# Strided rows loaded as two separate halves, fourteen weight tiles, and one memory for both score arrays

## The chip, the core and the metric

The kernel runs on one core of one Trainium2 chip. A core has five engines with their own instruction queues: TensorE (PE, with its weight loads as PEld), VectorE (DVE), ScalarE (ACT), GpSimd (POOL) and SyncE (SP). Data move between HBM and the on-chip SBUF through 16 DMA engines that all queues share. The metric is the device time of one execution in microseconds (us). Before the change it is 444.04 us, the median of four runs (443.17 to 445.94).

## The reference

```python
def _attn_ref(q, k, v):                      # 8 batches, 8 heads, 576 positions, 64 wide
    scores = scale * np.matmul(q, k.transpose(0, 1, 3, 2))
    rel = pos[:, None] - pos[None, :]
    mask_local = (rel >= 0) & (rel < 32)
    mask_strided = (rel >= 0) & (pos[None, :] % 32 == pos[:, None] % 32)
    masks = np.stack([mask_local if h < H // 2 else mask_strided for h in range(H)])
    ...
    return np.matmul(softmax(scores), v)

def _moe_ref(x, w_r, w_i, w_ch):             # x: the attention, 8 x 576 x 512
    X = np.fft.rfft(x, axis=1)
    ...
    # for each of 64 modes: Y = X (w_r + i w_i), with 512 x 512 matrices
    y = np.fft.irfft(Y, n=S, axis=1)
    u = x + y
    return u + np.maximum(u @ w_ch, 0.0)
```

Heads 0 to 3 attend to the last 32 positions ("local"), heads 4 to 7 to positions that are a multiple of 32 away ("strided"). The result goes through a Fourier transform, 64 complex 512 x 512 matrices (one for each mode), the inverse transform and one more matrix. All inputs are float32; the mode matrices alone are 134 MB, and the page counts 163.37 MB read from HBM.

## The kernel before

The kernel computes in 16-bit floats. Every load of q, k, v and of the mode matrices is a DMA that POOL issues and that turns float32 in HBM into float16 in SBUF. In the trace POOL has at most eight such DMAs under way: each names one of eight semaphores in turn, and waits for the DMA that used it before. SBUF destinations are tiles from pools with a fixed number of buffers, so an issue also waits until the tile's former contents have been read. POOL works its instructions strictly in order.

There are four stages.

1. **Strided heads**, batches 0 to 7. `load(i)` (L194) takes a buffer `qn` of three (tag `qn`) and fetches v, q and k of heads 4 to 7: 72 rows (4 heads x 18 blocks of 32 positions), each of 2048 numbers. The loop at L718 calls `load(b + 3)`, then `w_fetch` for some mode matrices, then the work of batch b: `str_front` of the next batch (transposes of 128 columns of `qn` by PE, `str_q` and `str_turn`, copies by DVE and ACT), `str_scores` (PE scores, ACT exponentials into the array `PS`), and `str_values` (PE, then `normalise` on DVE). `PS` is cleared once at L714.
2. **Local heads**, batches 0 to 7, with the same buffers `qn` (128 rows of 1152 numbers a load). The exponentials go into the array `PL`, which must be zero between the parts that are written; it is cleared at L734 after strided batch 1. Between pieces of this work stand the first halves of modes, `mode(0, m)`.
3. **Second halves of the modes**, `mode(1, m)`, with the work on the output matrix in between.
4. **Output**: the inverse transform, the last matrix, the additions and the stores.

A mode needs a tile `wt` (128 x 2048), filled by two DMAs of 64 rows, one from `w_r` and one from `w_i` (L180). `w_fetch` takes the next tile in order. There are `NWBUF` = 12 tiles in the pool `pw`; six tiles (numbers 3 to 6, 16 and 17) lie as guests in memory that other arrays use later. Before stage 2 the kernel fetches 2 tiles and then 3, 3, 2, 2, 2, 2, 1, 1 in the eight strided batches, 18 in all. After that each mode fetches one tile as soon as it is done (L523), except the modes whose tile was a guest in the first half. In the output stage the same pool gives the buffers `rl` and `osb`.

Of the kernel before, what the change touches and what calls it, by code (L numbers as in the profile page):

```python
# [11 lines left out]
F16 = mybir.dt.float16  # L12
# [11 lines left out]
JG = [(0, 6), (6, 11), (11, 16)]  # L24
SCALE = float(1.0 / np.sqrt(D))
NEG = -30000.0
NWBUF = 12


def _host_consts():  # L30
# [47 lines left out]
def kernel(  # L78
# [10 lines left out]
    nc = tc.nc  # L89
# [16 lines left out]
    def psum(kind, half=False):  # L106
        if half:
            return pss[kind].tile([128, 1024], F16, tag=kind, name=kind)
        return pss[kind].tile([128, 512], FP, tag=kind, name=kind)
# [27 lines left out]
    def spectra_tile(n):  # L137
        if n == "X0":
            Xh[0] = big.tile([128, 4, B, 2, NM], F16, tag=n, name=n)
        else:  # L140
            YS[n] = big.tile([128, 4, 4, 16, 16], F16, tag=n, name=n)

    xb = [px.tile([128, 11, 256], F16, tag="xb", name="xb") for _ in range(B)]

    pw = ctx.enter_context(tc.tile_pool(name="pw", bufs=NWBUF))
    actx = ctx.enter_context(ExitStack())
    pin = actx.enter_context(tc.tile_pool(name="pin", bufs=3))
    pat = actx.enter_context(tc.tile_pool(name="pat", bufs=1))
# [1 line left out]
    qTs = [pat.tile([128, 1152], F16, name=f"qT{i}") for i in range(2)]  # L150
    kzs = [pat.tile([128, 2, 1216], F16, name=f"kz{i}") for i in range(2)]
    vT = pat.tile([128, 1216], F16, name="vT")
    PS = pat.tile([128, 2342], F16, name="PS")
    PL = pat.tile([128, 4160], F16, name="PL")
    v16 = [pat.tile([128, 12, 132], F16, name=f"v16_{i}") for i in range(2)]


# [7 lines left out]
    def w_fetch(n=1):  # L165
        for _ in range(n):
            i = len(w_tiles)
            if i >= 2 * NM:
                return
            half, m = 1 - i // NM, i % NM  # L170
            if i in GUEST:
                n, j = GUEST[i]
                if j == 0:
                    guests[n] = big.tile([128, 2, 4, DM], F16, tag=n, name="wt")
                wt = guests[n][:, j]
            else:
                wt = pw.tile([128, 4, DM], F16, tag="w", name="wt")

            for ri, src in enumerate([moe_w_r, moe_w_i] if m else [moe_w_r]):
                nc.gpsimd.dma_start(  # L180
                    wt[ds(64 * ri, 64)],
                    src[m, ds(256 * half, 256), :].rearrange("(p c) e -> p c e", c=4),
                )
            w_tiles.append(wt)
# [4 lines left out]
        w_chs["n"] = w_ch  # L189


    qns = {}

    def load(i):  # L194
        if i >= 2 * B:
            return
        qn = pin.tile([128, 3, 2048], F16, tag="qn", name="qn")
        for vi, src in ((2, v), (0, q), (1, k)):
            if i < B:
                nc.gpsimd.dma_start(  # L200
                    qn[0:72, vi, :],
                    src[i, 4:8].rearrange("h (c r) d -> (h c) (r d)", r=32),
                )
            else:
                nc.gpsimd.dma_start(
                    qn[:, vi, 0:1152],
                    src[i - B, 0:4].rearrange("h (cb i) d -> (h cb) (i d)", i=18),
                )
        qns[i] = qn


    def v_cols(i):
        return ds(1 + 65 * i, 65)
# [13 lines left out]
    def act_copy(out, in_):  # L227
        nc.scalar.activation(out=out, in_=in_, func=ACTF.Copy)  # L228
# [4 lines left out]
    def str_q(b, g):  # L233
        qn, qT = qns[b], qTs[b % 2]
        tp = psum("tp", half=True)
        for i in range(8):
            nc.tensor.transpose(
                tp[:, ds(72 * i, 72)],
                qn[0:72, 0, ds(128 * (8 * g + i), 128)],
                idn[0:72, 0:72],  # L240
            )
        nc.vector.tensor_copy(
            out=qT.rearrange("p (h r c) -> p r h c", h=4, r=16)[:, ds(8 * g, 8)],
            in_=tp[:, 0:576].rearrange("p (r h c) -> p r h c", h=4, c=NCB),
        )

    def str_turn(b, vi, j):
        qn = qns[b]
        a, z = JG[j]
        nr = z - a  # L250
        tp = psum("tp", half=True)
        for i in range(nr):
            nc.tensor.transpose(  # L253
                tp[:, ds(72 * i, 72)],
                qn[0:72, vi, ds(128 * (a + i), 128)],
                idn[0:72, 0:72],
            )

        def move(eng, dst, pr):
            eng(  # L260
                out=dst[:, ds(72 * a, 72 * nr)].rearrange(
                    "p (h c r) -> p h c r", h=4, r=nr
                ),
                in_=tp[pr, 0 : 72 * nr].rearrange("p (r h c) -> p h c r", h=4, c=NCB),
            )

        if vi == 2:
            move(act_copy if j else nc.vector.tensor_copy, vT[:, 0:1152], ds(0, 128))
            return
        for rp in range(2):  # L270
            pr = ds(64 * rp, 64)
            move(
                act_copy if j == 1 else nc.vector.tensor_copy,
                kzs[b % 2][pr, rp, 0:1152],
                pr,
            )
# [29 lines left out]
    def str_scores(b, t):  # L306
# [13 lines left out]
        for h in range(4):  # L320
# [7 lines left out]
        nc.scalar.activation(  # L328
            out=PS[0:n, ds(POFF[t], 4 * n)],
            in_=scp[0:n, 0 : 4 * n],  # L330
# [4 lines left out]
    def str_values(b, t):  # L335
        vg = v16[b % 2]
        j, rp = STR[t]
        n = (JG[j][1] - JG[j][0]) * NCB
        avp = psum("av")
        av = avp[:, 0:264].rearrange("p (h c) -> p h c", c=66)  # L340
        for h in range(4):
            nc.tensor.matmul(
                av[:, h, 0:65],
                PS[0:n, ds(POFF[t] + n * h, 128)],
                vg[0:n, 4 * j + h, v_cols(rp)],
                start=True,
                stop=True,
            )
        normalise(
            av[0:n, :, ds(1 - rp, 64)],  # L350
            av[0:n, :, 64 * rp],
            n,
            4,
            xb[b][0:n, 3 * rp + j, :].rearrange("p (c h q) -> p h c q", c=4, h=4),
        )
# [49 lines left out]
    def loc_scores(b, h, tail):  # L405
# [18 lines left out]
        for i, (col, s0, n) in enumerate(todo):  # L424
# [6 lines left out]
            )  # L431
        PV = PL[:, 0:4096].rearrange("p (h x) -> p h x", h=4)
        if tail:
# [7 lines left out]
    def loc_values(b, h):  # L441
        vg = v16[b % 2]
        av = psum("av")[:, 0:330].rearrange("p (t c) -> p t c", c=66)
        for t in range(5):
            off = 1024 * h + (256 * t if t < 4 else 960)
            nc.tensor.matmul(
                av[:, t, 0:65],
                PL[:, ds(off, 128)],
                vg[:, 2 * t + h % 2, v_cols(h // 2)],
# [3 lines left out]
            if t > 0:  # L453
                nc.tensor.matmul(  # L454
                    av[:, t, 0:65],
                    PL[:, ds(1024 * h + 256 * t - 128, 128)],
                    vg[:, 2 * (t - 1) + h % 2, v_cols(h // 2)],
# [11 lines left out]
    def dft(b, half):  # L469
        if half == 0 and b == 0:  # L470
            spectra_tile("X0")
        xp = psum("sc" if half else "y")
        tiles = (
            [(t, (JG[t % 3][1] - JG[t % 3][0]) * NCB) for t in range(6)]
            if half
            else [(t, SCS[t]) for t in range(5)]
        )
        F = cs["cFs"] if half else cs["cFl"]
        base = 0 if half else 6
        for cp in range(2):  # L480
            for i, (t, n) in enumerate(tiles):
                nc.tensor.matmul(  # L482
                    xp[:, ds(192 * cp, 192)],
                    xb[b][0:n, base + t, ds(128 * cp, 128)],
                    F[0:n, t, :],
                    start=(i == 0),
                    stop=(i == len(tiles) - 1),
                )
        xv = xp[:, 0:384].rearrange("p (c x) -> p c x", c=2)
        X = Xh[half]  # L490
        for src in range(2):
            for dst in range(2):
                args = dict(
                    out=X[ds(64 * dst, 64), ds(2 * src, 2), b].rearrange(
                        "p c g m -> p c (g m)"
                    ),
                    in_=xv[ds(64 * src, 64), :, ds(64 - 64 * dst, 128)],
                )
                act_copy(**args)
# [179 lines left out]
    load(1)  # L679
    const_load(nc.sync, "cMl", "cFl", "cA")  # L680
    load(2)
    w_fetch(2)

# [22 lines left out]
    for i, w in enumerate(first):  # L706
# [6 lines left out]
        if i == 2:  # L713
            nc.vector.memset(PS, 0.0)  # L714
        if i == 5:
            nc.vector.memset(kzs[1], 0.0)
    SPLIT = [0, 2, 4, 5, 7, 8, 10]
    for b in range(B):  # L718
        load(b + 3)
        w_fetch([3, 3, 2, 2, 2, 2, 1, 1][b])  # L720
        front = str_front(b + 1) if b + 1 < B else loc_front(0)
        for t in range(6):
            str_scores(b, t)
            if b > 0:
                if t < 2:
                    str_values(b - 1, 4 + t)
                elif t == 2:
                    dft(b - 1, 1)
            if t >= 2:
                str_values(b, t - 2)  # L730
            for w in front[SPLIT[t] : SPLIT[t + 1]]:
                w()
        if b == 1:
            nc.vector.memset(PL, 0.0)  # L734
    str_values(B - 1, 4)
    str_values(B - 1, 5)
    dft(B - 1, 1)


# [179 lines left out]
    for i in range(len(units)):  # L919
        v_rows(i)  # L920
        b, t = units[i]
# [42 lines left out]
```

The softmax here doesn't subtract the row's maximum and nothing guards it: scores larger than these inputs give would overflow.

## Time and profile before

| | |
|---|---|
| median of four runs | 444.04 us (443.17 to 445.94) |
| the profiled execution | 445.94 us; its span, from the first to the last instruction, 444.1 us |
| PE, DVE, ACT, POOL busy | 77%, 49%, 43%, 41% of the span |
| mean granted TensorE clock | 0.801 |
| strided loads (L200) | 24 DMAs of 72 rows of 4096 B each |
| local loads (L205) | 24 DMAs of 128 rows of 2304 B each |
| weight loads (L180) | 254 DMAs of 64 rows of 4096 B each |

The sizes are those written to SBUF; twice as much is read. The profile's page divides the span into 40 slices of 11.1 us and gives the busy share of each engine in tenths, the mean busy share of the 16 DMA engines, and the rate in GB/s as written. A DMA share can be a little above 1 in the windows, since successive packets of an engine overlap. The chain of waits follows the work that ended last back from the end, and gives for each step what released it; time in which an engine waited for a transfer is put down to that transfer.

### The profile page before, as it was taken

The numbers are of one execution on the slowest core, as the hardware profiler recorded it, in microseconds if no ns is written. First come the engines' busy times: TensorE is split into PE (matmuls) and PEld (weight loads), VectorE is DVE, ScalarE is ACT, GpSimd is POOL, SyncE is SP. The second block draws the span as 40 slices with busy tenths as digits, with TensorE's granted clock in tenths as the row PEclk, the third lists the DMA queues.
The fourth block names the chain that finished last, engine by engine and source line by source line (L and its number), as shares of the span: only waits on it lengthen the run. The fifth ranks groups of instructions, "written<-read, shape, count | busy, mean of one in ns | idle before, by whom it ended". The sixth has DMA issues, their size and how long they took to land.

```text
span 444.1 us, 12290 instructions
## 1 busy us (share of the span) xinstructions
PE 341.8 (77%) x5284; PEld 244.1 (55%) x5284; DVE 215.8 (49%) x462; ACT 188.9 (43%) x353; POOL 180.6 (41%) x327
## 2 busy tenths in 40 slices
PE   3887787869979897876865566768587958997994
PEld 2766676758767775654653344445455535554441
DVE  4788776833535425150511033354345443763895
ACT  2686676743545554343341302133222402433882
POOL 5243343332544343434443444444344444410883
PEclk9998897975887959595885559596867768988998
DMA  8999999999999999999999999999999999991687
GB/s 186 183 204 205 196 199 208 209 208 206 165 211 211 212 212 211 212 211 213 212 211 212 211 212 212 213 212 213 211 200 213 212 211 211 212 203 21 261 318 274
DMA packets 30902, 92.35 MB, mean 208 GB/s; under 512 B 5952, under 2 KB 6848, under 8 KB 30848
## 3 DMA queue, kind: packets, MB, share of 16 engines
q0 software_dynamic: 26608, 81.28, 93.6%
q1 hardware_dynamic: 3440, 9.50, 5.7%
q8 instruction: 42, 0.69, 0.6%
q10 hardware_dynamic: 800, 0.77, 0.6%
q14 instruction: 12, 0.10, 0.1%
HBM read 163.37 MB, written 9.44 MB: 389 GB/s over the span
## 4 chain that ended last, share of the span: by engine, by line
DMA 57%; PE 27%; DVE 9%; issue 4%; ACT 2%; DVEq 0%; POOL 0%; POOLq 0%
DMA wt<-in_moe_w_i_dram 40%; DMA wt<-in_moe_w_r_dram 9%; DMA qn<-in_q_dram 4%; PE y L515 4%; PE sc L613 3%; DMA qn<-in_v_dram 3%; DMA qn<-in_k_dram 2%; PE v L860 2%; DVE xb L218 2%; PE tp L363 2%; PE v L648 2%; PE u L663 2%; DVE kz L260 2%; PE sc L409 1%; PE sc L482 1%
## 5 line engine op out<-in xcount | busy, mean ns | idle before, releaser
L515 PE MATMUL y<-X,wt 128*128 128x16 f16 (+1 forms) x2048 | 82.9, 192 | 62.5 <-DMA wt<-in_moe_w_i_dram 58.0
L180 POOL DMA_DIRECT2D wt<-in_moe_w_r_dram x128 | 66.2, 517 | 129.6 <-DMA wt<-in_moe_w_r_dram 35.0
L515 PEld LDWEIGHTS <-wt 128*128 128x128 f16 (+1 forms) x2048 | 72.9, 103 | 75.4 <-issue 55.2
L180 POOL DMA_DIRECT2D wt<-in_moe_w_i_dram x126 | 65.1, 517 | 64.9 <-DMA wt<-in_moe_w_i_dram 39.4
L622 ACT ACTIVATE v<-sc 128x512 f16<-128x512 f32 x32 | 18.9, 597 | 88.7 <-PE sc L613 88.6
L613 PE MATMUL sc<-w_cp,xT 128*128 128x512 f16 (+1 forms) x160 | 52.8, 461 | 0.5 <-DVE xT L585 0.4
L439 ACT ACTIVATE PL<-sc 128x480 f16<-128x480 f32 (+1 forms) x48 | 27.6, 579 | 39.2 <-PE sc L425 39.0
L623 DVE COPY xo<-tp 128x512 f16<-128x512 f16 x32 | 22.1, 692 | 41.4 <-PE tp L621 41.4
L218 DVE TENSOR_TENSOR xb<-av,rec 90x256 f16<-90x256 f32 (+2 forms) x80 | 36.0, 450 | 2.7
L217 DVE RECIPROCAL rec<-av 90x4 f32<-90x4 f32 (+2 forms) x80 | 14.7, 184 | 45.1 <-PE av L454 31.5
L370 DVE COPY qT<-tp 128x576 f16<-128x576 f16 x16 | 12.0, 758 | 44.9 <-PE tp L363 40.7
L228 ACT ACTIVATE v<-tp 128x640 f16<-128x640 f16 (+1 forms) x24 | 19.4, 808 | 28.9 <-PE tp L397 26.0
L363 PE MATMUL tp<-cI_s,qn 64*64 64x64 f16 x864 | 25.9, 209 | 2.1 <-issue 1.0
L873 POOL TENSOR_TENSOR rl<-rl,xo 128x512 f32<-128x512 f32 x16 | 18.3, 1157 | 20.2 <-ACT rl L871 19.5
L328 ACT ACTIVATE PS<-sc 90x360 f16<-90x360 f32 (+1 forms) x48 | 22.8, 488 | 8.2 <-PE sc L321 7.6
L890 DVE TENSOR_TENSOR osb<-u,rl 128x512 f32<-128x512 f32 x36 | 23.8, 689 | 3.1 <-ACT rl L871 1.4
L363 PEld LDWEIGHTS <-qn 64*64 64x64 f16 x864 | 20.4, 121 | 7.4 <-issue 4.4
L253 PE MATMUL tp<-cI_s,qn 72*128 72x72 f16 x256 | 15.1, 209 | 11.8 <-DMA qn<-in_v_dram 9.4
L409 PE MATMUL sc<-cMl_s,cI_s 128*128 128x480 f16 (+1 forms) x48 | 22.5, 470 | 1.6 <-ACT X L228 1.6
L482 PEld LDWEIGHTS <-xb 108*128 108x128 f16 (+2 forms) x176 | 17.0, 114 | 11.4 <-DVE xb L218 5.7
L613 PEld LDWEIGHTS <-xT 128*128 128x128 f16 (+1 forms) x160 | 14.8, 111 | 15.0 <-issue 7.4
L565 DVE COPY xT<-tp 128x512 f16<-128x512 f16 x16 | 11.0, 689 | 24.3 <-DMA wt<-in_moe_w_i_dram 15.2
(94 smaller groups left out, 660.0 us busy)
## 6 DMA issues: line engine op xcount, KB each, us to landing
wt<-in_moe_w_r_dram POOLq DMA_DIRECT2D x128, 256.0 KB, 9.5
wt<-in_moe_w_i_dram POOLq DMA_DIRECT2D x126, 256.0 KB, 9.7
out_dram<-osb SPq DMA_DIRECT2D x14, 512.0 KB, 2.7
qn<-in_v_dram POOLq DMA_DIRECT2D x16, 288.0 KB, 10.3
qn<-in_q_dram POOLq DMA_DIRECT2D x16, 288.0 KB, 10.7
qn<-in_k_dram POOLq DMA_DIRECT2D x16, 288.0 KB, 10.8
out_dram<-osb SPq DMA_DIRECT2D x7, 128.0 KB, 2.5
out_dram<-osb SPq DMA_DIRECT2D x3, 256.0 KB, 2.6
```

The source lines that it names most:

```text
L180: nc.gpsimd.dma_start(wt[ds(64 * ri, 64)], src[m, ds(256 * half, 256), :].rearrange("(p c) e -> p c e", c=4),)
L218: nc.vector.tensor_tensor(out=dst, in0=val.rearrange("p h (q c) -> p h c q", c=4), in1=rec[0:n, 0:pieces] .to_broadcast((n, pieces, 64)) . ...
L228: nc.scalar.activation(out=out, in_=in_, func=ACTF.Copy)
L328: nc.scalar.activation(out=PS[0:n, ds(POFF[t], 4 * n)], in_=scp[0:n, 0 : 4 * n], func=ACTF.Exp, scale=SCALE,)
L363: nc.tensor.transpose(tp[ds(64 * hp, 64), ds(64 * i, 64)], qn[ds(64 * hp, 64), vi, ds(64 * (9 * g + i), 64)], idn[ds(64 * hp, 64), ds(64 * ...
L409: nc.tensor.matmul(scp[:, 0 : n * times].rearrange("p (h x) -> p h x", h=times), idn, mask_rows("cMl", n, times), start=True, stop=False,)
L439: nc.scalar.activation(out=dst, in_=src, func=ACTF.Exp, scale=SCALE)
L482: nc.tensor.matmul(xp[:, ds(192 * cp, 192)], xb[b][0:n, base + t, ds(128 * cp, 128)], F[0:n, t, :], start=(i == 0), stop=(i == len(tiles) ...
L515: nc.tensor.matmul(yv[:, mi, e, :], wt[pr, XC[c], ds(128 * e, 128)], Xh[half][pr, c, :, :, m], start=(c == 0), stop=(c == 3),)
L613: nc.tensor.matmul(vp[pr, :], xT[:, ch, cols], w_chs["cp"][:, ch, :], start=(ch == 0), stop=(ch == 3),)
L623: nc.vector.tensor_copy(out=xo[pr].rearrange("p (h q c) -> p h q c", h=2, c=4), in_=tp[pr, 0:512].rearrange("p (h c q) -> p h q c", h=2, c=4),
L890: nc.vector.tensor_tensor(out=osb[:, t % 2, :], in0=up, in1=rls[b, t][:, t % 2, :], op=AluOp.add)
```

## The change

It has three parts. A strided row of 2048 numbers is no longer one piece: the buffer `qn` grows from 2048 to 2080 columns, and the second half of a row starts at column 1040 in place of 1024, so that the two halves don't adjoin in SBUF. The load's pattern is now 72 x 2 x 1024, and `pair_cols` gives the transposes their columns. The pool of weight tiles has 14 buffers, and batches 6 and 7 of the strided stage fetch two tiles each in place of one; 20 tiles are fetched before stage 2. `PS` is no array of its own but the last 2342 columns of `PL`: the clearing at L734 covers only the first 1818 columns, and a second one clears the others after the last strided values.

```diff
-NWBUF = 12
+NWBUF = 14
...
-    PS = pat.tile([128, 2342], F16, name="PS")
+
     PL = pat.tile([128, 4160], F16, name="PL")
+    PS0 = 4160 - 2342
+    PS = PL[:, ds(PS0, 2342)]
...
+    HALF = 1024 + 16
     qns = {}
+
+    def pair_cols(i):
+        return ds(HALF * (i // 8) + 128 * (i % 8), 128)
...
-        qn = pin.tile([128, 3, 2048], F16, tag="qn", name="qn")
+        qn = pin.tile([128, 3, 2 * HALF], F16, tag="qn", name="qn")
...
-                    qn[0:72, vi, :],
-                    src[i, 4:8].rearrange("h (c r) d -> (h c) (r d)", r=32),
+                    qn[0:72, vi, :].rearrange("p (f x) -> p f x", f=2)[:, :, 0:1024],
+                    src[i, 4:8].rearrange("h (c f r) d -> (h c) f (r d)", f=2, r=16),
...
-                qn[0:72, 0, ds(128 * (8 * g + i), 128)],
+                qn[0:72, 0, pair_cols(8 * g + i)],
...
-                qn[0:72, vi, ds(128 * (a + i), 128)],
+                qn[0:72, vi, pair_cols(a + i)],
...
-        w_fetch([3, 3, 2, 2, 2, 2, 1, 1][b])
+        w_fetch([3, 3, 2, 2, 2, 2, 2, 2][b])
...
-            nc.vector.memset(PL, 0.0)
+            nc.vector.memset(PL[:, 0:PS0], 0.0)
     str_values(B - 1, 4)
     str_values(B - 1, 5)
+    nc.vector.memset(PS, 0.0)
     dft(B - 1, 1)
```

In the order of the instructions nothing else moves: PE has the same instructions in the same order, DVE has the one memset more, and POOL issues the two added tile fetches (four DMAs) ahead of the loads of local batches 2 and 3.

## The prediction

> **What bounds the kernel now.** I read the page's slices first, then the chain of waits, then the windows by stage, then the POOL timeline where a stage lost transfer time.
>
> ```profile
> DMA  8999999999999999999999999999999999991687
> GB/s 186 183 204 205 196 199 208 209 208 206 165 211 211 212 212 211 212 211 213 212 211 212 211 212 212 213 212 213 211 200 213 212 211 211 212 203 21 261 318 274
> q0 software_dynamic: 26608, 81.28, 93.6%
> ...
> DMA wt<-in_moe_w_i_dram 40%; DMA wt<-in_moe_w_r_dram 9%; DMA qn<-in_q_dram 4%; PE y L515 4%; PE sc L613 3%; DMA qn<-in_v_dram 3%; DMA qn<-in_k_dram 2%; PE v L860 2%; DVE xb L218 2%; PE tp L363 2%; PE v L648 2%; PE u L663 2%; DVE kz L260 2%; PE sc L409 1%; PE sc L482 1%
> ```
>
> From slice 2 to slice 36 the DMA engines are at 90% or more, and the chain that ends last lies for 40 + 9 + 4 + 3 + 2% of the span in transfers that POOL issues. In order of time the chain runs through DMA from 50 to 73 us (the strided rows of the last batches), through the compute engines from 73 to 134, through weight transfers from 134 to 373, and from 373 through the last modes and the output stage, 71 us that follow the weights of mode 51 whenever those land. So the time is the 16 engines' transfer work up to about 373 us, plus whatever they lose before that. The windows (columns: busy PE, PEld, DVE, ACT, POOL; granted clock; DMA share; GB/s) show where they lose:
>
> ```profile
> 20.00:30.00 10.00, 8.27 (x149) 6.80 (x147) 8.65 (x25) 8.16 (x19) 3.13 (x7) 1.00 1.04 202
> 50.00:60.00 10.00, 7.54 (x114) 6.52 (x113) 6.66 (x19) 6.34 (x15) 3.75 (x8) 0.83 1.03 195
> 110.00:114.00 4.00, 4.00 (x95) 3.90 (x92) 1.93 (x5) 1.73 (x3) 1.78 (x4) 0.52 0.67 125
> 260.00:330.00 70.00, 52.22 (x679) 33.80 (x679) 27.97 (x55) 14.92 (x26) 27.88 (x55) 0.75 1.06 212
> ```
>
> Weights alone run at 212 GB/s. The stage with strided rows (up to 70 us) runs at 195 to 206, and at 110 to 114 us the rate falls to 125.
>
> **Part 1: the strided rows.** Each of the 24 strided loads has 72 rows of 4096 B. The page's packet count says how they are dealt out. Queue 0 has 26608 packets. Data rows are 254 x 64 weight rows, 24 x 72 strided, 24 x 128 local and 512 of `w_ch`: 21568. The 5040 left are completion packets of 4 B. 303 DMAs with 16 engines each make 4848; the other 192 are 24 x 8. So every strided load carries eight fillers: 72 + 8 = 80 = 16 x 5. The trace's landing records agree: of a load's 16 increments two come early (the first q load: 4.88 and 6.13 us) and fourteen together (7.90 to 8.41 us). Fourteen engines take five rows, one takes two, one none, and the loaded engines set the pace. In the packet records successive packets on one engine start 304.5 ns apart at 4096 B, 173 at 2304 and 79 at 1024; these lie on a line of 73.4 ns per 1000 B plus 3.9 ns, so 2048 B is estimated at 154.2 ns.
>
> After the change a load is 144 pieces of 2048 B. If the 144 are dealt out as the 72 were, each engine gets exactly nine. Per load the busiest engine goes from 5 x 304.5 = 1522.5 to 9 x 154.2 = 1387.8 ns, 134.7 less, times 24 loads = **-3.2 us**. The whole is on the path if the engines had no other cause of idling then; for the first nine loads (start and constants) that is not clear, so the smaller bound is 15 x 134.7 ns = 2.0.
>
> Here the Trainium skill speaks against the change ("DMA: Bandwidth & Descriptors", "Why a DMA increments its semaphore by 16 and not by 1"): the number of engines comes from the slowest dimension, and some copies from GpSimd get 16 engines with partitions/16, rounded up, on each. The row agrees for 72 x 1, where pieces and partitions are the same, and can't tell them apart. Read by partitions, 72 x 2 still gives five partitions, ten pieces, to fourteen engines: 10 x 154.2 = 1542 ns, 24 x 19.5 = +0.5 us in place of -3.2. I take dealing by pieces, because the fillers pad the pieces to a multiple of 16 and the pattern has no other trace of partitions; both ends stay in the range.
>
> POOL's side: an issue takes 526 ns for 72 rows, 531 to 566 for 128, 782 for the 512 pieces of `w_ch`, so about 570 for 144: 24 x 40 ns = 1 us of POOL. It lies beside POOL's own waits for earlier transfers (the view of waits: 50 us each before `w_r` and `w_i` issues), so nothing; without that cover, 1 us. The transposes read other columns at the same count and width: nothing.
>
> **Part 2: two more weight tiles.**
>
> ```profile
> 104.25 0.52 POOL L180 DMA_DIRECT2D wt<-in_moe_w_i_dram  x1
> 111.76 0.52 POOL L180 DMA_DIRECT2D wt<-in_moe_w_r_dram  x1 [6.99 <-PE y L515]
> ```
>
> This is the hole at 110 us. By 97 us all 18 tile slots (12 and six guests) are filled; modes 3 to 6 free guest tiles and fetch nothing, so POOL issues nothing for 7 us and the queue runs dry. The loss is 4 x (1 - 125/212) = 1.6 us. With 14 tiles two more fetches (batches 6 and 7) stand ahead of the hole: 4 DMAs x 4 rows per engine x 304.5 = 4.9 us of work. Part 1 takes 3.2 us from the same queue, so it runs dry 1.7 us later, about the size of the hole; if PE reaches mode 7 earlier, because the strided rows came earlier, the cover is better. I take **-1.5 us** (bounds 0.5 and 1.6; up to 0.9 more if the 179 GB/s just behind the hole, 114 to 120 us, is its consequence). Total bytes are the same: the two tiles come earlier, not additionally. What is late next: from 134 us on the weights again; PE does a mode of the local stage in some 1.7 us (22 modes from 97 to 134) against 2.4 us of transfer, so it eats the lead and then waits as before.
>
> Queued behind the two fetches are POOL's loads of local batches 2 and 3 (issued at 86.4 and 94.0). They slip by 2.4 and 4.9 us less what part 1 gives, and land near 100 and 109 us; their transposes start in the rounds of local batches 1 and 2, after 112 us: nothing. The pool is also that of the output stage's `rl` and `osb`; no row of the waits has these waiting for an output transfer, so two more buffers give nothing there.
>
> **Part 3: the scores' shared memory.** The memset at L734 shrinks from 1.79 us (2080 words) to 1818/4160 of it, 0.78; on DVE in batch 1, a stretch in which the chain goes on to wait for DMA at 50 us, so nothing. A memset of 1171 words is added after the last strided values: 1.03 us by the row of the same memset at L714 (7.84 us). It starts behind the last normalise (94.4 + 0.4 us) and ends near 95.9; the first local exponential, which now waits for it, runs at 98.32 because its scores wait for the copies of X, and DVE's next instruction comes at 98.95 after 4.1 idle us. So 0; uncovered, 1.0 us.
>
> **Sum.** -3.2 - 1.5 + 0 = -4.7 us. The profiled execution took 445.94 (span 444.1 and 1.8 around it), so it would take 441.2. It is the longest of the four; against the median of 444.04 the forecast is **439.3 us**, -1.1%.
>
> **Rivals.** (a) *Dealt by partitions.* Part 1 is +0.5, the hole is covered in full: -1.6 + 0.5 = -1.1, so 442.9, which can't be told from no change. For it: the skill's wording. Against: the fillers. (b) *Twelve engines.* The other branch of the same rule gives 72 rows the largest divisor up to 16, which is 12; today's loads don't follow it, but two-dimensional ones might. Then a used engine gets 12 pieces, 1850 ns. If the twelve move on from load to load, the mean is nine again and the forecast holds. If they are always the same, each load costs 328 ns more than now: 24 x 0.328 = +7.9, less 1.6: 450.3, slower. It decides from the point where the busiest engine's share of a load exceeds 1522.5 + 1640/24 = 1591 ns, that is 10.3 pieces. Nothing in today's loads speaks for it; the one two-dimensional load, `w_ch`, has 128 partitions and does not tell. The same point is reached if 2 KB pieces cost over 177 ns each, which the 173 ns of 2304 B speaks against. (c) *The loads stay hidden*: if compute sets the pace to 134 us, balance only fills buffers sooner. But that is what the two tiles absorb, and from 134 us the time is transfer work; without it only part 2 would remain, 442.5.
>
> **The numbers.** Forecast, with moving twelves, 0.63; (a) with (c) 0.25; (b) and other losses 0.12. What can be told from no change is 0.5%, 2.2 us: below 441.8 is faster. The forecast's own range is 437.5 to 441.5 (-3.0 to -5.7, and a run's scatter), so nine tenths of it are faster; of (a) a fifth. Faster 0.57 + 0.05 = 0.62, slower 0.12, the rest 0.26. Range 437.5 to 443.8: up through (a) and its scatter, leaving out (b).
>
> **What would show it.** Dealing: queue 0 would have 16256 + 3456 + 3072 + 512 + 4848 = 28144 packets without fillers; 28528 with sixteen per load says (a). The windows from 20 to 70 us should rise from 195-206 to about 210 GB/s, and the two early increments of each load go. The hole: no window of 4 us under 200 GB/s between 105 and 120, and no 7 us of idle POOL that empties the queue. The last weights should land near 397 instead of 402 us, with the 42 us behind them unchanged. A strided stage that is no faster than now would make the first step wrong; a hole that only moves would make the second wrong; local exponentials that wait for DVE, the third.

## The result and the profile after

| | before | after |
|---|---|---|
| median | 444.13 us (64 runs, 442.58 to 446.66) | 444.49 us (43 runs, 441.54 to 448.75) |
| profiled execution | 445.94 us, span 444.1 | 445.08 us, span 443.3 |
| PE, DVE, ACT, POOL busy | 77%, 49%, 43%, 41% | 77%, 49%, 42%, 42% |

The ratio of the times after and before is 1.0008, with a 95% interval of 0.9997 to 1.0018: no change that can be told. The forecast was 439.3 us. The longest of the 43 runs, 448.75 us, counts as a slow one and is left out of the ratio. These are the lines of the changed kernel's page that answer to those shown before:

```profile
DMA  8999999999999999999999999999999999990687
GB/s 172 182 192 204 203 204 208 211 212 212 212 211 213 210 210 201 211 209 215 210 213 209 211 211 213 212 213 210 211 193 211 211 212 212 211 207 15 262 320 274
q0 software_dynamic: 29296, 81.29, 95.3%
...
DMA wt<-in_moe_w_i_dram 44%; DMA qn<-in_v_dram 5%; DMA qn<-in_q_dram 5%; DMA wt<-in_moe_w_r_dram 4%; PE y L524 4%; PE sc L622 3%; PE v L870 2%; PE v L657 2%; DVE xb L227 2%; PE tp L372 2%; PE u L672 1%; DVE kz L269 1%; PE sc L491 1%; PE sc L418 1%; PE sc L434 1%
```

Three things are to be seen. The slice that stood at 165 GB/s (the eleventh, 111 to 122 us) is at 212: the hole is gone. The first four slices, which held 186 183 204 205, hold 172 182 192 204, and the next two, which held 196 199, hold 203 204: the start got slower, and the rest of the strided stage hardly faster. And the queue has 29296 packets, neither the 28144 nor the 28528 that the prediction had named. The chain is of the same make as before, with 44 + 5 + 5 + 4% of the span in transfers that POOL issues; the transfers still set the end. The windows of the changed kernel (busy PE, PEld, DVE, ACT, POOL; granted clock; DMA share; GB/s) say the same more sharply:

```profile
10.00:20.00 10.00, 7.03 (x83) 6.22 (x84) 6.50 (x11) 4.11 (x8) 3.54 (x6) 1.00 1.27 178
20.00:70.00 50.00, 41.88 (x674) 35.36 (x672) 38.81 (x108) 35.59 (x78) 21.27 (x37) 0.90 1.12 200
110.00:114.00 4.00, 4.00 (x70) 3.49 (x68) 1.37 (x4) 1.79 (x4) 1.51 (x3) 0.66 1.08 214
260.00:330.00 70.00, 52.82 (x678) 33.89 (x674) 28.29 (x56) 15.28 (x26) 27.39 (x54) 0.71 1.06 211
```

The kernel before, in the same stretches:

```profile
10.00:20.00 10.00, 8.34 (x117) 7.28 (x116) 6.88 (x16) 5.65 (x10) 3.11 (x6) 1.00 1.07 184
20.00:70.00 50.00, 39.20 (x658) 32.79 (x656) 39.64 (x107) 36.15 (x80) 18.53 (x37) 0.93 1.04 201
```

From 20 to 70 us the rate is the same, 200 against 201 GB/s, but the DMA share rose from 1.04 to 1.12. The share counts the time for which packets are open; for the same bytes they are open longer. The records of the single packets agree: 2048 B has a median of 173 ns (successive starts 154 ns apart, as estimated), but a mean of 196 ns, and in the microseconds behind each group of strided loads the mean of one microsecond peaks at 220 to 284 ns.

**How the loads are dealt out.** By size, the queue's packets are 16256 of 4096 B, 3456 of 2048 B, 3072 of 2304 B, 512 of 1024 B and 6000 of 4 B. 303 DMAs with 16 completions each make 4848 of the small ones; 1152 are left, 48 for each of the 24 strided loads. 48 = 4 x 12: four engines get twelve 4-byte fillers each, and twelve engines get 144 / 12 = 12 pieces. The landing records agree: of the first v load's 16 increments four come at 4.76 to 5.24 us, and twelve at 6.45 to 8.52. An increment does not name its engine, but engines that are left out every time run ahead: in the kernel before, two of the increments of the seventh load come at 7.40 and 11.10 us and fourteen at 17.30 to 18.07. In the changed kernel all sixteen of the seventh load come at 17.04 to 19.20, so the twelve move on. That is the other branch of the rule that the prediction quoted from the Trainium skill ("DMA: Bandwidth & Descriptors", "Why a DMA increments its semaphore by 16 and not by 1"): the largest number up to 16 that divides the slowest dimension, here 12 of 72, on consecutive engines from a cursor that goes round. The count of twelve and the moving on agree with it; no run here shows that the engines are consecutive. The loads of the kernel before (72 x 1) follow its exception instead, rounded-up shares on 16 engines, with their eight fillers. In both cases the fillers bring every engine up to the largest share: 3 + 5 where one engine has two rows of five and one has none, 4 x 12 here.

**What this did at the start.** The first strided loads landed later: v at 8.5 us in place of 6.2, q at 11.3 in place of 8.4, and the first exponential runs at 17.4 in place of 14.6. The lead of the transfers over those of the kernel before (difference of the bytes of queue 0 begun so far, at 212 GB/s) was -0.7 us at 5 us, -1.5 at 40 and -0.4 at 110. It became +1.25 at 114 and +2.2 at 120 through the hole that is no longer there, and +0.8 at 372; 0.6 and 0.5 us of it went at about 172 and 326 us, where POOL stops (last section). The profiled execution before was 1.8 us longer than its kernel's median and this one 0.6 longer than its own, so the small lead left at the end fits a ratio of 1.

### The profile page after: what moved, and what is told of

It reads as the page before. It is cut to its first block, busy times and chain, and to the rows that moved or that the text cites. A ratio compares the mean times of both kernels' runs of the same rounds, so it can differ in the third digit from the quotient of the medians.

```text
span 443.3 us, 12287 instructions
## 1 busy us (share of the span) xinstructions
PE 339.1 (77%) x5284; PEld 242.6 (55%) x5284; DVE 216.0 (49%) x463; ACT 188.2 (42%) x353; POOL 184.9 (42%) x327
## 3 DMA queue, kind: packets, MB, share of 16 engines
q0 software_dynamic: 29296, 81.29, 95.3%
## 4 chain that ended last, share of the span: by engine, by line
DMA 58%; PE 27%; DVE 9%; issue 4%; ACT 2%; POOL 0%; DVEq 0%; ACTq 0%; POOLq 0%
DMA wt<-in_moe_w_i_dram 44%; DMA qn<-in_v_dram 5%; DMA qn<-in_q_dram 5%; DMA wt<-in_moe_w_r_dram 4%; PE y L524 4%; PE sc L622 3%; PE v L870 2%; PE v L657 2%; DVE xb L227 2%; PE tp L372 2%; PE u L672 1%; DVE kz L269 1%; PE sc L491 1%; PE sc L418 1%; PE sc L434 1%
## 5 line engine op out<-in xcount | busy, mean ns | idle before, releaser
L622 PE MATMUL sc<-w_cp,xT 128*128 128x512 f16 (+1 forms) x160 | 51.9, 454 | 0.5 <-DVE xT L594 0.4
L337 ACT ACTIVATE PL<-sc 90x360 f16<-90x360 f32 (+1 forms) x48 | 22.8, 490 | 8.1 <-PE sc L330 7.5
L434 PE MATMUL sc<-qT,kz 128*128 128x160 f16 (+1 forms) x160 | 22.4, 267 | 0.0
```

The source lines that it names most:

```text
L337: nc.scalar.activation(out=PS[0:n, ds(POFF[t], 4 * n)], in_=scp[0:n, 0 : 4 * n], func=ACTF.Exp, scale=SCALE,)
L434: nc.tensor.matmul(scp[:, ds(col, n)], kzs[par][:, hp, ds(s0, 128)], qTs[par][:, ds(s0, n)], start=False, stop=(i == len(todo) - 1),)
L622: nc.tensor.matmul(vp[pr, :], xT[:, ch, cols], w_chs["cp"][:, ch, :], start=(ch == 0), stop=(ch == 3),)
```

## The experiments

The theory was from here on: **the dealing**. A load whose pieces go unevenly over the 16 engines is slow, although the shares even out over several loads; the two tiles bring a little and the halves take it back. The first rival was that 2 KB pieces themselves are slow, whatever their dealing; the second, that only the late first loads cost time. Each kernel was timed beside the kernel before; the ratio is to that, with its 95% interval.

### One part at a time

Tiles and shared score memory alone: the changed kernel with rows loaded whole (24 loads of 72 x 2048).

```diff
-    HALF = 1024 + 16
+    HALF = 1024
...
-                    qn[0:72, vi, :].rearrange("p (f x) -> p f x", f=2)[:, :, 0:1024],
-                    src[i, 4:8].rearrange("h (c f r) d -> (h c) f (r d)", f=2, r=16),
+                    qn[0:72, vi, :],
+                    src[i, 4:8].rearrange("h (c r) d -> (h c) (r d)", r=32),
```

> The changed kernel with whole strided rows again: only the 14 tiles and the shared score memory are left. Theory (the tiles gain, the halves give it back): the hole at 110 to 114 us is gone and nothing is lost at the start, 1.5 to 2.5 us faster than before (441.6 to 442.6). Rival (neither part matters, the hole is hidden anyway): 444 within 0.5 us, although the hole is gone.

Measured: 443.78 us in 22 runs against 444.34, ratio 0.9985 [0.9972, 0.9998].

Halves alone: the kernel before (12 tiles, two score arrays) with only the halved loads.

> The kernel before with nothing but the strided rows in two separate halves. Theory (the halves cost at the start what they give later, or more): transfers behind the kernel before by 1 to 1.5 us at 40 us and the hole at 110 us still there; 444 to 446. Rival (neither part matters): 444 within 0.5 us. My prediction's first step, if it was right after all: 441.

Measured: 444.75 us, ratio 1.0020 [1.0001, 1.0040]. Tiles -0.7 us and halves +0.9 us by the ratios, +0.2 together; the change as a whole is +0.36. The parts add up, and each is small. The tiles missed the expected 441.6 to 442.6. In the tiles' profile the hole is covered at the same low clock (0.50) at which the kernel before had it:

```profile
20.00:70.00 50.00, 38.08 (x664) 31.60 (x660) 38.51 (x106) 36.14 (x79) 18.75 (x36) 0.93 1.04 201
110.00:114.00 4.00, 4.00 (x95) 3.90 (x93) 1.59 (x5) 1.90 (x3) 1.40 (x3) 0.50 1.07 213
```

213 GB/s where there were 125, and a lead of 2.4 us at 120 us in this one profile; yet the median moved by 0.7 only.

### Is it only the start?

The halves only from batch 3 on; the nine loads of batches 0 to 2 stay whole.

```diff
+    WHOLE = 3
...
-            if i < B:
+            if i < WHOLE:
+                nc.gpsimd.dma_start(
+                    qn[0:72, vi, 0:2048],
+                    src[i, 4:8].rearrange("h (c r) d -> (h c) (r d)", r=32),
+                )
+            elif i < B:
```

> The changed kernel, with whole rows for the loads of strided batches 0 to 2, which stand at the start, and halves from batch 3 on. Theory (the loss of the halves lies in the start alone, and later they give about 70 ns a load): 1 us better than the tiles alone, 440.5 to 441.5. Rival (halves cost in every load): the same as the changed kernel or 0.5 us above the tiles alone.

Measured: 443.49 us, ratio 0.9979 [0.9966, 0.9992], which the intervals don't tell from that of the tiles alone (0.9985). The expected 440.5 to 441.5 was missed: against the whole change (1.0008) the restored early loads give back 0.3%, 1.3 us, so what the halves cost lies in the main at the start; but the later halves still bring nothing. The windows of this kernel show why:

```profile
20.00:70.00 50.00, 40.90 (x614) 34.62 (x611) 36.48 (x100) 33.87 (x75) 20.68 (x36) 0.83 1.12 197
28.00:30.00 2.00, 1.32 (x29) 1.11 (x28) 1.61 (x5) 1.90 (x5) 0.00 (x0) 1.00 1.26 164
62.00:64.00 2.00, 1.02 (x21) 0.71 (x18) 1.89 (x6) 1.53 (x4) 0.61 (x1) 1.00 1.30 161
```

Behind groups of strided loads the rate falls to 161 to 164 GB/s while the DMA share is 1.26 to 1.30. The late start explains the cost, not why the forecast gain stays away in the later loads.

### Smaller pieces

Four quarters of 1024 B that do not touch (`HALF` becomes 512 + 16, four to a row), with the tiles.

> The changed kernel with each strided row in four separate quarters of 1024 B in place of two halves. If the 4 B filler packets cost transfer time, they double from 48 to 96 a load (queue 0: 29296 + 3456 + 1152 = 33904 packets), and with pieces of 79 ns a load costs some 24 x 79 ns = 1.9 us on each used engine in place of 1.85: about 1.5 to 3 us slower than the changed kernel (446 to 447.5), most of it before 40 us, since issues take still longer. Rival (fillers and issues are hidden): 444.5 as the changed kernel.

Measured: 447.27 us in five runs, ratio 1.0067 [1.0041, 1.0092]. The packet count, 33904, has 7152 of 4 B: 4848 and 24 x 96, which is 4 x 24. So the filler rule holds: twelve engines, and as many fillers on each of the other four as a used engine has pieces. The time lies in the expected range, but its reason isn't borne out: the transfers of this profile led those of the kernel before by 1.5 us at 372 us, the rate from 20 to 70 us was 202 GB/s, and the last steps of the chain stand where they did in the changed kernel, down to its last link, on DVE's sequencer (DVEq) behind the last addition. First the changed kernel's chain, then that of the quarters (start, length, what):

```profile
437.26 0.87 DVEq L969
```

```profile
437.35 0.87 DVEq L969
```

The span nevertheless ends at 444.6 instead of 443.3 us. So nearly all of the 1.3 us by which this profile is longer lie behind the last addition; the medians differ by 2.8, and the rest isn't seen in it. This stays open.

### How large is the hole?

The kernel before, profiled a second time.

> The kernel before once more, for a second profile. The first one is of an execution 1.8 us above the median. If the hole at 110 to 114 us is the same in every execution: again about 125 GB/s there and 7 us in which POOL issues nothing. If its size hangs on the clock that PE is granted (0.52 there in the first profile): a smaller hole where the clock is higher, and a gain of the two tiles below 1.6 us.

Measured: 445.02 us in this one execution. POOL's timeline in the first profile of the kernel before had an idle time of 6.99 us behind the issue at 104.25. In the second one (start, length, engine, line; in brackets the idle time before and what ended it):

```profile
105.26 0.52 POOL L180 DMA_DIRECT2D wt<-in_moe_w_i_dram  x1 [0.60 <-DMA qn<-in_v_dram]
109.94 0.52 POOL L180 DMA_DIRECT2D wt<-in_moe_w_r_dram  x1 [4.16 <-PE av L454]
```

And the windows, as before, with that of 100 to 110 us in the first profile ahead:

```profile
100.00:110.00 10.00, 10.00 (x204) 8.34 (x203) 4.32 (x8) 3.92 (x7) 2.82 (x6) 0.50 1.08 209
```

```profile
100.00:110.00 10.00, 9.31 (x252) 7.93 (x250) 5.03 (x10) 4.57 (x8) 2.86 (x7) 0.95 1.09 211
110.00:114.00 4.00, 3.96 (x81) 3.23 (x81) 1.32 (x4) 2.43 (x5) 3.04 (x6) 1.00 1.01 194
```

4.16 us of idle POOL in place of 6.99, and 194 GB/s in place of 125: the loss in that window is 4 x (1 - 194/212) = 0.3 us, not 1.6. What differs is PE's granted clock while POOL waits for PE to be done with a tile, 0.95 here and 0.50 there. The halves alone, also with 12 tiles, fit: at 0.90 POOL was idle for 3.22 us, and the window from 110 to 114 us held 201 GB/s. So the size of the hole differs from execution to execution; that the clock sets it fits these profiles, of which one alone had the low clock.

### Equal shares for 16 engines

If the dealing is the cause, the same halves dealt evenly must bring what was forecast. 64 rows go evenly over 16 engines (eight pieces each); the other eight rows become a DMA of their own, whose 8 x 2 pieces take eight engines that move on from load to load. First only from batch 3 on, then everywhere:

```diff
-                nc.gpsimd.dma_start(
-                    qn[0:72, vi, :].rearrange("p (f x) -> p f x", f=2)[:, :, 0:1024],
-                    src[i, 4:8].rearrange("h (c f r) d -> (h c) f (r d)", f=2, r=16),
-                )
+                for p0, n in ((0, 64), (64, 8)):
+                    nc.gpsimd.dma_start(
+                        qn[ds(p0, n), vi, :].rearrange("p (f x) -> p f x", f=2)[
+                            :, :, 0:1024
+                        ],
+                        src[i, 4:8].rearrange(
+                            "h (c f r) d -> (h c) f (r d)", f=2, r=16
+                        )[ds(p0, n)],
+                    )
```

> As the version with halves from batch 3 on, but each of those loads is two DMAs: rows 0 to 63 in halves, and rows 64 to 71 in halves. Theory (the slow packets behind each strided burst come from dealing 144 pieces to twelve engines; 128 pieces go evenly to sixteen): no fillers for the 64 rows, 16 for the eight, the rate between 25 and 75 us rises to 205 GB/s and more, with no second under 180, and 0.5 to 1 us better than halves from batch 3: 442.5 to 443. Rival (the slow packets come from short pieces, or from strided rows in whatever form): the same slow seconds, 443.5 or, with the added issues, slower.

> The changed kernel with every strided load as two such DMAs, from the start. Theory: the start is later than in the changed kernel or as late (two issues a load, eight DMAs under way are only four loads), the rest better: 444 to 445. Rival: 445 to 446, as the added issues cost in every load.

Measured: 441.83 us (ratio 0.9954 [0.9935, 0.9974]) and **439.92 us** (0.9913 [0.9886, 0.9939]), against 444.17. Both are better than was expected (442.5 to 443, and 444 to 445): the late start that the second expectation counted on did not come, as the window from 10 to 20 us below shows. The rival of slow 2 KB pieces falls: these are the same pieces in the same SBUF places. The page and the windows of the second kernel:

```profile
q0 software_dynamic: 28912, 81.29, 95.0%
```

```profile
10.00:20.00 10.00, 8.70 (x123) 7.78 (x122) 7.37 (x18) 5.61 (x10) 7.66 (x15) 1.00 1.12 207
20.00:70.00 50.00, 39.69 (x684) 33.28 (x682) 40.72 (x112) 38.27 (x84) 28.20 (x52) 0.97 1.09 210
110.00:114.00 4.00, 4.00 (x120) 3.38 (x116) 2.43 (x5) 1.74 (x3) 1.53 (x4) 1.00 1.06 213
```

28912 less 16256 + 3456 + 3072 + 512 is 5616 = 327 x 16 + 24 x 16: the eight-row load has 16 fillers, the 64-row load none. The stage runs at 210 GB/s at a lower share (1.09) than the changed kernel's 200 at 1.12, and the mean of a 2048 B packet is 174 ns in place of 196. The weights' packets of 4096 B, which are the same in both kernels, show it too: from 20 to 70 us their mean is 345 ns in the changed kernel and 324 here, as in the stretch with weights alone (324 to 326 ns in both from 260 to 320 us). All 16 increments of the first v load's 64 rows come together, at 5.65 to 6.50 us, and its last eight rows are there at 7.35, in place of 8.52. POOL's part rises, from 24 issues of mostly 685 ns to 48 of about 575 ns, 21.27 to 28.20 us of POOL from 20 to 70 us, without harm. The last weights come about 6 us earlier, as the rate by slices of 1.2 us from 372 us on shows; the changed kernel first, then the even shares:

```profile
GB/s 208 212 208 218 212 205 219 208 215 212 208 222 198 215 215 212 212 212 208 212 215 212 113 55 10 0 0 0 14 0 0 0 177 266 58 386 355 273 331 382
```

```profile
GB/s 215 212 215 215 208 208 208 215 212 215 215 212 201 215 222 201 212 116 102 89 3 0 14 0 0 15 328 108 79 358 379 260 341 379 171 208 328 372 232 389
```

The full rate ends with the 22nd slice (398.4 us) in the one and with the 17th (392.4 us) in the other.

### Is it the count of DMAs, or the halves?

Two more kernels, and the best one again. One has the 64 + 8 division with whole rows and 14 tiles. Its landings say that a DMA of eight whole rows uses the same eight engines each time: eight of the 16 increments come at 13.57 to 14.02 us in one DMA, the other eight at 14.70 to 14.99, and this gap grows, to 1.2 us in the DMA that lands at 18 us.

> The tiles alone, with each strided load as two DMAs of whole rows, 64 and 8. Theory (only an even share for each of the sixteen engines helps; eight whole rows always go to the same eight engines, which then take five rows as now): 0 to 0.5 us from the tiles alone, about 443.8 us, and a strided stage at about 200 GB/s. Rival (two smaller DMAs a load help by themselves, or the halves did nothing in the fast version): 440, strided stage at 210 GB/s.

Measured: 442.43 us, ratio 0.9966 [0.9949, 0.9983], between the theory (443.8) and its rival (440); by the ratios 0.8 us better than 72 whole rows with 14 tiles (0.9985), with intervals that overlap. Its windows:

```profile
10.00:20.00 10.00, 8.70 (x127) 7.76 (x125) 7.42 (x18) 5.75 (x11) 6.77 (x14) 1.00 1.05 198
20.00:70.00 50.00, 39.78 (x670) 33.92 (x668) 39.77 (x108) 36.69 (x81) 25.24 (x50) 0.93 1.05 203
```

From 20 to 70 us the rate is 203 GB/s, not 210, and the mean of a 4096 B packet there is 333 ns: more and smaller DMAs alone do not do it, the halves on moving engines are needed. By the ratios they bring 2.0 us over this kernel (0.9920 in the last run below). The 198 GB/s at the start, against 181 with 72 whole rows, the theory did not foresee, and its cause is open.

The other has the even halves with the kernel before's 12 tiles and two score arrays.

> The kernel before with only the strided loads dealt evenly (64 and 8 rows, both in halves): 12 tiles and the scores' own memory as before. Theory (dealing is worth 3 us or more by itself; with the transfers ahead, 12 tiles are full earlier and the hole grows): 441 to 442, with a window from 105 to 115 us under 190 GB/s, 1 to 2 us behind the version with 14 tiles. Rival (the tiles add nothing): 440, as with 14 tiles.

Measured: 442.38 us, ratio 0.9959 [0.9939, 0.9979], with 210 GB/s from 20 to 70 us. POOL still stands idle for 4.7 us, from 101.3 to 106.0, at a clock of 1.00: transfers that run ahead fill the 12 tiles sooner.

```profile
106.00 0.51 POOL L180 DMA_DIRECT2D wt<-in_moe_w_r_dram  x1 [4.72 <-PE av L464]
```

But the expected window under 190 GB/s did not come: from 105 to 115 us the rate is 204. This profile is of one of the shortest of 22 executions (440.38 us, where they reach 446.29), and its transfers lead those of the kernel before by 5.6 us at 372 us, as in the profile of the next run (5.7). So the median's distance from that run isn't seen in it.

> The changed kernel with every strided load as 64 and 8 rows in halves, once more, timed in more rounds beside the other two: 439.5 to 440.5 if the first measurement holds.

Measured: 440.55 us in five runs (440.11 to 441.17), ratio 0.9920 [0.9905, 0.9935]. The gain stands. So the two tiles are worth 0.7 us with whole rows and 442.38 - 440.55 = 1.8 us once the loads run ahead; and even halves are worth 1.9 us with 12 tiles (444.24 to 442.38) and 0.9985 - 0.992 = 0.65%, 2.9 us, with 14. That each part is worth more beside the other is not clear of the noise: singly they give 0.15% and 0.41%, together 0.80%, and the intervals are 0.13 to 0.20% wide to either side.

## Why the prediction was wrong

**Dealing (part 1).** The failed step is the sentence "I take dealing by pieces, because the fillers pad the pieces to a multiple of 16", with nine pieces for each of 16 engines. 72 x 1, the only shape that the trace showed, could not tell pieces from partitions, as the text itself said; the new shape went to twelve engines. The eight fillers were no padding to a multiple of 16: they bring every engine up to the largest share, which for 72 x 1 comes to the same number. Rival (b) had that right. But its escape, "if the twelve move on from load to load, the mean is nine again and the forecast holds", fell too, and with it the forecast: they do move on, and the part measured +0.9 us in place of -3.2. Within a load a used engine has twelve pieces; the first loads land later (v at 8.5 in place of 6.2 us), and packets are open longer (196 against 174 ns). The gain came when 128 of a load's 144 pieces were dealt evenly and the other 16 to eight engines that move on; why uneven shares stretch the packets stays open. The other half of (b), 450.3 us for always the same twelve, did not occur, and rival (a), 28528 packets, did not either.

Where the balance exists, the size of the gain is near the forecast's 3.2: over the tiles alone the even halves bring about 3.0 us (the tiles' ratio of 0.9985 against 0.9913 and 0.9920). But the arithmetic is not confirmed by that: the division of whole rows into 64 and 8 leaves five rows on the busiest engines and yet brought perhaps 0.8 of it, and the halves 2.0. The times of the even kernel, 439.92 and 440.55, lie near the forecast of 439.3 us, but its gain by the ratios is 3.6 to 3.9 us where 4.7 was forecast.

**Issue cost (part 1).** An issue was estimated at 570 ns and took 685, the first one 871. The three loads at the start stand one behind the other on POOL, so this adds to the late first landings; there, "so nothing" may have been too little. It can't be the most of them: the even halves spend more on issues there (two of about 575 ns a load), and their first q load lands at 9.1 us where that of the changed kernel lands at 11.3. How much of the 0.9 us it is wasn't separated.

**The hole (part 2).** The mechanism was right: no window under 200 GB/s at 110 to 120 us, no idle POOL of 7 us. The size was off: -1.5 us forecast, -0.7 measured with whole rows. It was read from one execution with a low clock at that place; the second, at 0.95 to 1.00, lost 0.3 us there. Rival (c), 442.5 us with only part 2 working, carried the same size: tiles alone took 443.78.

**Memory (part 3).** Right: the first local exponential ran at 97.9 us, 98.3 before, and waited for PE's scores, not for the memset.

**The marks.** "About 210 GB/s" from 20 to 70 us was 200; the last weights at 397 instead of 402 us came less than 1 us earlier. Each of these shows the first step wrong without the time. The range ended at 443.8 us and so left (b) out.

## What to carry to other kernels

Count the packets and the 4-byte fillers of a queue: here they told over how many engines a DMA was dealt, and a change of shape changed that number. Try equal shares for all 16 engines within each DMA, the remainder as a DMA of its own whose engines move on; in this kernel an average over loads that was even wasn't enough. And size a stall from more than one profile, with the granted clock beside it.

## What the runs showed of the hardware

- The fillers follow the shape: 72 x 1 has 8 a load, 72 x 2 has 48, 72 x 4 has 96, 64 x 2 none, 8 x 2 has 16, 8 x 1 has 8. One rule gives all six: every engine is filled up to the largest share. Most fillers take 22 ns.
- Packets stretched in the kernels whose strided loads were all uneven: the mean of 2 KB packets rose to 284 ns in single microseconds, at DMA shares of 1.2 to 1.3 and 161 to 175 GB/s, and from 20 to 70 us 4 KB packets took 333 to 348 ns in the mean, in the three profiles with even halves throughout 324 to 325. Why, and whether HBM or the way into SBUF causes it, was not tried.
- POOL's issue goes by shape: 526 ns for 72 x 1, 685 for 72 x 2, 566 to 585 for 64 x 2 and 8 x 2.
- POOL stops for 3.9 us behind its 128th and its 249th DMA (171.5 to 175.4 and 326.0 to 329.9 us in the changed kernel: the slices at 201 and 193 GB/s). In all profiles but that of the quarters it stops behind the same counts, for 3.4 to 4.1 us; the quarters stop once, behind the 217th. The cause isn't shown.
